# Turning the softmax blocks inside SBUF instead of through DRAM, in a fused attention and gMLP kernel

## The chip, the cores and the metric

The kernel runs on one core of a Trainium2 chip. The time is device microseconds of one execution; three executions of the kernel before gave 1901.39, 1904.52 and 1908.22 us, so the median is 1904.52 us. The engines are TensorE (PE, with its weight loads as PEld), VectorE (DVE), ScalarE (ACT), GpSimd (POOL) and SyncE (SP), which here only issues DMAs. Each engine runs its own instructions in order and waits on semaphores for the others.

## The reference

The input x (2048 x 512) is normalised by rows. Two branches read it: attention with 32 heads over the last 512 keys of a cache, and a gMLP block. The output is x plus the attention times silu of the gMLP.

```python
def _A_ref(x, k_cache, v_cache, wq, wo):
    W = min(4096, max(256, Sk // 4))                     # 512
    q = (x @ wq).reshape(B, Sq, Hq, Dh).transpose(0, 2, 1, 3)
    scores = einsum("bhqd,bhkd->bhqk", q, k_last_W) * Dh ** -0.5
    p = softmax(scores)
    o = einsum("bhqk,bhkd->bhqd", p, v_last_W)
    return o.transpose(0, 2, 1, 3).reshape(B, Sq, Hq * Dh) @ wo

def _B_ref(x, w_in, w_sp, b_sp, w_out):
    z = gelu(x @ w_in); z1 = z[..., :Fh]; z2 = layernorm(z[..., Fh:])
    g = einsum("ts,bsf->btf", w_sp, z2) + b_sp[None, :, None]
    return (z1 * g) @ w_out

xn = layernorm(x)
return x + _A_ref(xn, ...) * silu(_B_ref(xn, ...))
```

## The kernel before, in words

Everything is fp32. A product of two fp32 matrices is made of three matmuls in a fast fp32 format: each operand is split into a high part (a cast on ACT, tile names ending in `_h`) and the rest (a subtraction on DVE or POOL, names ending in `_l`), and `mm3` (lines 64 to 67) issues high x high, high x low and low x high.

**The main loop.** The attention works in 128 blocks: one head by 512 queries. A block has four steps of 128 queries, so there are 512 steps, and the program is written out by hand step by step: every engine's order is the order in which the loop at the end of the printed code calls the functions. For a block b the work is spread over many steps, each part a fixed number of steps behind the scores:

- `score(t)`: PE makes the scores of step t in a PSUM tile `ps` (pool of four), DVE finds the negated maximum `nm`, ACT makes `prob` = exp(scores + nm) with its row sums.
- `turn(t-1)`, one step later: p must have keys on partitions to be multiplied with v. DVE's transpose turns 32 x 32 pieces within a partition group only, so the groups of 32 partitions must still be exchanged. Before, the transposed pieces of two steps stand in a tile `pB`, which SP writes to DRAM (`p_dram`, 512 KB, two writes per block), and `turned(b)`, called in step 4b+7, reads it back with its groups exchanged in four transfers of 256 KB into `pL`.
- `shares(b, c)`, in step 4b+11+c (`ML` = 11): ACT casts a quarter of `pL` into `pT_h`, POOL makes `pT_l`.
- `pv(b, c)`, in step 4b+13+c (`PL` = 13): three matmuls add p times v into a PSUM bank `ps_a`; after the fourth, `pv_out` splits the sum into `oT_h` and `oT_l`.
- `outp(b, j)`, in step 4b+18+j (`OL` = 18): three matmuls with wo, and DVE adds the result, divided by the row sums, into `sacc`.

**The queries** for four blocks together, a group, are made by 42 matmuls spread over 16 steps (`q_products`, line 448), which begin `LEAD` = 13 steps ahead of the group's first score. They use three banks, a, b and c: bank b holds one product in the third to the fifth of the 16 steps, bank c two from the eighth step on, and bank a is kept for all 16 steps and let go by `qT_l` (line 728, the deferred list `late` at the end of a step) one step after the next group's products have begun. The group's banks and the banks of `pv` come from one pool of four PSUM banks, named `ps_a`; a tile of that name gets the bank that is free or the first to become free.

**SP** issues the loads of weights (`raw`, `wq`, 256 KB each, two per block on average), stores and loads of the normalised x (`x_dram`), the writes of p and the reads of p, in the order of the program. A DMA that has to wait for DVE or POOL holds up all DMAs behind it. The DMAs take eight completion semaphores in turn, and each one waits, before it is issued, until the one that had its semaphore before it, eight DMAs earlier, has landed (the waits named DMAHW in the rows further down).

Between steps 30 and 215 the second half of x is normalised, transposed and split (`later_x`), in stages that go through a ring of four tiles `rawx`; ACT writes a tile of the ring again when its store to `x_dram` has landed.

After the loop come the second half of the gMLP's first product and its spatial product (from about 1560 us on), which this change does not touch.

Of the kernel before, what the change touches and what calls it, by code (L numbers as in the profile page):

```python
# [8 lines left out]
F32 = mybir.dt.float32  # L9
F32R = mybir.dt.float32r  # L10
# [7 lines left out]
P = 128  # L18
# [10 lines left out]
NBLK = H * NQ  # L29
# [1 line left out]
SCALE = DH ** -0.5  # L31


XL, QL, ML, PL, OL = 11, 7, 11, 13, 18
T8 = NT // 2
LEAD = 13
Q = 32


# [1 line left out]
def mixer_kernel(ctx: ExitStack, tc: tile.TileContext, x, wh, w_in, w_sp, b_sp, w_out, out):  # L41
# [8 lines left out]
    nc = tc.nc  # L50
# [3 lines left out]
    dram = ctx.enter_context(tc.tile_pool(name="dram", bufs=1, space=DRAM))  # L54
# [3 lines left out]
    def rest(engine, lo, whole, hi):  # L58
        engine.tensor_tensor(lo, whole, hi.bitcast(F32), op=OP.subtract)  # L59

    late = []
# [25 lines left out]
    ap = att.enter_context(tc.tile_pool(name="ap", bufs=2))  # L87
# [6 lines left out]
    def x8(shape, dtype=F32R):  # L94
        return xp.tile(shape, dtype, name="x8")
# [18 lines left out]
    def place(key, k, early):  # L114

        if early:
            if key == ("w", 0) or k == 3:
                name = "pT" if key == ("w", 0) else "oT"
                return [ap.tile([P, 512], F32R, name=f"{name}_{a}", bufs=4 if name == "pT" else 2) for a in "hl"]
            f = (1, 2, 2)[k]  # L120
        elif key[0] == "h":
            f = k
        elif key[0] == "q":
            f = 3
        elif key[1] < 2:
# [234 lines left out]
    def z1_piece(i, n, between=lambda: None):  # L360
        z1_out(i, n, z1_product(i, n, between))


    pB = [None]
    qps, qT, pps, pD, pL, pT, oT, prob, sums = {}, {}, {}, {}, {}, {}, {}, {}, {}

    def where(b):

# [36 lines left out]
    def load_q(g):  # L405
        r = wraw[g] = wq.tile([P, 2, 512], F32, name="wq", bufs=2)
        h = 2 * g % H
        for k in range(2):
            nc.sync.dma_start(r[:, k], wh[h + k, :, 0])
# [69 lines left out]
    def turn(t):  # L479

        b, j = divmod(t, 4)
        if j % 2 == 0:
            pB[0] = ap.tile([P, 4, 2, P], F32, name="pB", bufs=3)
        nc.vector.transpose(pB[0][:, :, j % 2, :].rearrange("p a (c q) -> p a c q", q=Q),  # L486
                            prob.pop(t).rearrange("p (a c q) -> p a c q", a=4, q=Q))
        if j == 0:
            pD[b] = dram.tile([2, P, 1024], F32, name="p_dram", bufs=3)
        if j % 2:  # L490
            nc.sync.dma_start(pD[b][j // 2], pB[0].rearrange("p a j f -> p (a j f)"))
        if j == 3:
            nc.vector.reciprocal(sums[b], sums[b])

    def turned(b):
        pL[b] = ap.tile([P, 8, 256], F32, name="pL")
        of = pD.pop(b).rearrange("s (i r) (a f) -> a r (s i) f", i=4, a=4)
        for a in range(4):
            nc.sync.dma_start(pL[b][Q * a:Q * a + Q], of[a])

    def shares(b, c):
        hi = ap.tile([P, 512], F32R, name="pT_h", bufs=4)
        lo = ap.tile([P, 512], F32R, name="pT_l", bufs=4)
        p = pL[b].rearrange("p i (j f) -> p (i j) f", j=2)[:, :, Q * c:Q * c + Q]
        h, l = (t.rearrange("p (i q) -> p i q", q=Q) for t in (hi, lo))
        nc.scalar.copy(h, p)  # L506
        rest(nc.vector if 4 * b + c >= NSTEP - 10 and c % 2 else nc.gpsimd, l, p, h)
        pT[b, c] = (hi, lo)
# [6 lines left out]
    def pv_out(b, c):  # L515
        if c == 3:
            hi = ap.tile([P, 512], F32R, name="oT_h")
            lo = ap.tile([P, 512], F32R, name="oT_l")
            ps = pps.pop(b).rearrange("p (s i j q) -> p s i j q", s=2, i=4, j=2)
            h, l = (t.rearrange("p (s j i q) -> p s i j q", s=2, i=4, j=2) for t in (hi, lo))  # L520
            nc.scalar.copy(h, ps)
            for k in range(2):
                late.append((rest, nc.vector, l[:, k], ps[:, k], h[:, k]))
            oT[b] = (hi, lo)

    def outp(b, j):
# [44 lines left out]
    for g in range(1, NG):  # L571
        t0 = 16 * g - LEAD
        loads.setdefault(max(T0, t0 - 12), []).append(g)
# [72 lines left out]
    ps = ps_step.tile([P, 512], F32, name="ps_3")  # L646
# [9 lines left out]
    ps = ps_step.tile([P, 512], F32, name="ps_3")  # L656
# [4 lines left out]
    ps = ps_acc.tile([P, 512], F32, name="ps_a")  # L661
# [18 lines left out]
    for t in range(T0, T1):  # L680
        for key in loads.get(t, ()):
            if isinstance(key, int):
                load_q(key)
            else:
                load_piece(*key)
        bq, cq = divmod(t + QL, 4)
        bm, cm = divmod(t - ML, 4)
        bp, cp = divmod(t - PL, 4)
        bo, jo = divmod(t - OL, 4)
        i = t + XL  # L690
        if i < T8:
            ln_flip(i)
        if 0 <= bm < NBLK:
            shares(bm, cm)
        for f, args in todo.get(t, ()):
            f(*args)
        if 0 <= t < NSTEP:
            score(t)
        if i + 2 < T8:
            ln_apply(rows[i + 2], i + 2)  # L700
        if t in FILL:
            z1_piece(*FILL[t])
        if 0 <= bq < 4:
# [12 lines left out]
        for f, *args in q_events.get(t, ()):  # L716
            f(*args)
        if 0 <= bp < NBLK:
            pv_out(bp, cp)
        if t in DRAIN:  # L720
            z1_out(*DRAIN[t], ps)
        if 0 <= t - 1 < NSTEP:
            turn(t - 1)
        if t % 4 == 3 and 0 <= t // 4 - 1 < NBLK:
            turned(t // 4 - 1)
        while late:
            f, *args = late.pop(0)
            f(*args)  # L728
        for f, *args in ends.get(t, ()):
            f(*args)  # L730

    split_piece(("w", 2), 3, nc.vector)
    ps = z1_product(*LAST[-1])
# [276 lines left out]
```

## Time and profile before

| | |
|---|---|
| median of 3 runs | 1904.52 us (1901.39 to 1908.22) |
| profiled execution | 1907.01 us, its span 1905.1 us |
| mean granted TensorE clock of that execution | 0.991 |
| PE busy | 1820.5 us (96%) |
| DVE, POOL, ACT busy | 1403.3, 1244.3, 1179.1 us |
| DMA | 429.16 MB, mean 225 GB/s; queue of SP 79.4% of 16 engines |
| first and last maximum of scores (DVE, line 475) | 47.9 us, 1497.2 us |

The page gives shares of the whole span; the stages differ. The main loop is the stretch from about 60 to 1500 us, and in it a group of 16 steps takes 43.4 us where nothing disturbs it. In the rows of waits, "PE ps_a L65 <- DVE qT_l L728" means that PE stood idle before a matmul of line 65 that writes `ps_a`, until DVE's instruction of line 728 that writes `qT_l` had ended. PEld, the weight load, shows the same waits once more. A wait of an engine other than PE matters only where PE ends up waiting for it.

### The profile page before, as it was taken

Reading aid. Unit: us, or ns where it says so; the run is one execution under the profiler, and the core shown is the slowest. Engines: PE = TensorE matmul, PEld = TensorE weight load, DVE = VectorE, ACT = ScalarE, POOL = GpSimd, SP = SyncE. Lnnn points to the kernel's source line nnn. Section 1 sums busy time; section 2 is a strip of 40 time slices with the busy share of each in tenths; the row PEclk is TensorE's granted clock in tenths of the full one; section 3 lists DMA queues with packets and bytes.
Section 4 is the critical chain, followed back from the end, with each engine's and each line's share of the span. In section 5 each row is a group of like instructions: output and inputs, shape, how many; then the busy total and the mean of one; then the engine's idle time right before and its main releaser. Section 6 shows DMA issues by size and latency. Waiting matters only on the chain.

```text
span 1905.1 us, 28198 instructions
## 1 busy us (share of the span) xinstructions
PE 1820.5 (96%) x8658; PEld 1540.4 (81%) x8658; DVE 1403.3 (74%) x2497; ACT 1179.1 (62%) x2631; POOL 1244.3 (65%) x1185
## 2 busy tenths in 40 slices
PE   8898999999999898999999999999999999999999
PEld 7776777777787686778887877878777899999998
DVE  5687888888888787788888888888888556333433
ACT  4666677777677575667677777777677545333422
POOL 3686798798798786788878888888888435000000
PEclk9998999999999999999999999999999999999999
DMA  5798999999999889999889899988999833545543
GB/s 180 198 282 228 237 264 242 251 265 239 252 264 244 216 248 296 267 270 247 236 239 241 241 241 245 245 237 245 236 246 260 257 134 119 194 146 168 158 134 96
DMA packets 277624, 429.16 MB, mean 225 GB/s; under 512 B 22272, under 2 KB 183808, under 8 KB 276320
## 3 DMA queue, kind: packets, MB, share of 16 engines
q1 hardware_dynamic: 272864, 421.72, 79.4%
q10 hardware_dynamic: 4608, 5.64, 0.8%
q8 instruction: 68, 1.11, 0.3%
q14 instruction: 84, 0.69, 0.1%
HBM read 260.55 MB, written 166.72 MB: 224 GB/s over the span
## 4 chain that ended last, share of the span: by engine, by line
PE 73%; DMA 11%; DVE 7%; ACT 3%; POOL 3%; issue 2%; SPq 1%; ACTq 0%; POOLq 0%; DVEq 0%
PE ps_a L448 11%; PE ps L65 9%; PE ps L67 9%; PE ps L66 9%; PE ps_a L65 7%; PE ps_a L66 6%; PE ps_a L67 6%; DMA pL<-p_dram 4%; PE ps_g L66 4%; PE ps_g L67 4%; PE ps_g L65 4%; DMA p_dram<-pB 2%; DVE sacc L536 2%; DVE pB L486 1%; ACT prob L477 1%
## 5 line engine op out<-in xcount | busy, mean ns | idle before, releaser
L59 POOL TENSOR_TENSOR pT_l<-pL,pT_h 128x512 fp32r<-128x512 f32 x507 | 657.9, 1298 | 265.5 <-ACT pT_h L506 250.7
L477 ACT ACTIVATE prob<-ps,nm 128x512 f32<-128x512 f32 x512 | 352.8, 689 | 290.9 <-DVE nm L475 285.1
L536 DVE SCALAR_TENSOR_TENSOR sacc<-ps,sums,sacc 128x512 f32<-128x512 f32 x496 | 369.6, 746 | 149.2 <-PE ps L67 144.2
L506 ACT CAST pT_h<-pL 128x512 fp32r<-128x512 f32 x512 | 318.1, 621 | 130.8 <-DMA pL<-p_dram 68.3
L448 PE MATMUL ps_a<-x,x 128*128 128x512 f32 x1302 | 378.6, 391 | 7.9 <-ACT qs L455 6.9
L486 DVE STREAM_TRANSPOSE pB<-prob 128x512 f32<-128x512 f32 x512 | 359.0, 701 | 23.2 <-ACT prob L477 22.4
L475 DVE TENSOR_REDUCE nm<-ps 128x1 f32<-128x512 f32 x512 | 338.8, 662 | 8.6 <-PE ps L67 8.5
L448 PEld LDWEIGHTS ps_a<-x,x 128*128 128x128 f32 x1302 | 245.9, 189 | 61.9 <-ACT qs L455 8.3
L59 POOL TENSOR_TENSOR wl<-raw,wh 128x512 fp32r<-128x512 f32 x192 | 249.2, 1298 | 9.0 <-ACT wh L141 9.0
L65 PE MATMUL ps_a<-pT_h,wh 128*128 128x512 f32 x512 | 204.2, 399 | 46.7 <-DVE qT_l L728 42.3
L65 PE MATMUL ps<-wh,qT_h 128*128 128x512 f32 x512 | 204.0, 399 | 8.6 <-DVE sacc L536 5.1
L66 PE MATMUL ps_a<-pT_l,wh 128*128 128x512 f32 x512 | 203.0, 396 | 7.3 <-POOL pT_l L59 7.1
L67 PE MATMUL ps_a<-pT_h,wl 128*128 128x512 f32 x512 | 200.9, 392 | 0.0
L66 PE MATMUL ps<-wl,qT_h 128*128 128x512 f32 x512 | 200.9, 392 | 0.0
L65 PE MATMUL ps<-wh,oT_h 128*128 128x512 f32 x512 | 200.7, 392 | 0.0
L66 PE MATMUL ps<-wl,oT_h 128*128 128x512 f32 x512 | 200.6, 392 | 0.0
L67 PE MATMUL ps<-wh,oT_l 128*128 128x512 f32 x512 | 200.6, 392 | 0.0
L67 PE MATMUL ps<-wh,qT_l 128*128 128x512 f32 x512 | 200.6, 392 | 0.0
L66 PE MATMUL ps_g<-z_l,x 128*128 128x344 f32 x512 | 162.1, 317 | 1.3 <-POOL z_l L59 1.3
L65 PE MATMUL ps_g<-z_h,x 128*128 128x344 f32 x512 | 162.1, 317 | 0.0
L67 PE MATMUL ps_g<-z_h,x 128*128 128x344 f32 x512 | 161.9, 316 | 0.0
L65 PEld LDWEIGHTS ps_a<-pT_h,wh 128*128 128x128 f32 x512 | 96.7, 189 | 79.2 <-DVE qT_l L728 55.0
(203 smaller groups left out, 3235.3 us busy)
## 6 DMA issues: line engine op xcount, KB each, us to landing
p_dram<-pB SPq DMA_DIRECT2D x256, 512.0 KB, 5.2
pL<-p_dram SPq DMA_DIRECT2D x512, 256.0 KB, 5.8
raw<-wh SPq DMA_DIRECT2D x194, 256.0 KB, 6.7
wq<-wh SPq DMA_DIRECT2D x62, 256.0 KB, 6.1
x<-w_sp SPq DMA_DIRECT2D x60, 256.0 KB, 6.0
x_dram<-rawx SPq DMA_DIRECT2D x32, 256.0 KB, 5.6
x<-x_dram SPq DMA_DIRECT2D x28, 256.0 KB, 7.6
u_dram<-uB SPq DMA_DIRECT2D x15, 384.0 KB, 2.3
```

What stands on the lines that cost most here:

```text
L59: engine.tensor_tensor(lo, whole, hi.bitcast(F32), op=OP.subtract)
L65: nc.tensor.matmul(ps, lh, rh, start=first, stop=False)
L66: nc.tensor.matmul(ps, lh, rl, start=False, stop=False)
L67: nc.tensor.matmul(ps, ll, rh, start=False, stop=last)
L448: nc.tensor.matmul(qps[g, bank], wt["q", g, k][a][:, c * P:(c + 1) * P], X[g * 2 // H][ORDER[k]][:, b, c], start=first, stop=r == 5, skip_ ...
L475: nc.vector.tensor_reduce(nm, ps, axis=AX.X, op=OP.max, negate=True)
L477: nc.scalar.activation(prob[t], ps, AF.Exp, bias=nm, accum_out=sums[b][:, j:j + 1])
L486: nc.vector.transpose(pB[0][:, :, j % 2, :].rearrange("p a (c q) -> p a c q", q=Q), prob.pop(t).rearrange("p (a c q) -> p a c q", a=4, q=Q))
L506: nc.scalar.copy(h, p)
L536: nc.vector.scalar_tensor_tensor(at, ps, rs, at, op0=OP.mult, op1=OP.add)
```

## The change

p is turned without DRAM. The transposed pieces of all four steps of a block now stand in one `pB` (two buffers of 8 KB per partition, where there were three of 4 KB), and when the fourth is there, in step 4b+4, SP issues 16 transfers of 64 KB (32 partitions by 2 KB) from `pB` straight into `pL`, one for each pair of a source group and a target group. `turned` is gone. The casts come 9 steps behind the scores and no longer 11, `pv` 11 and no longer 13, `outp` 16 and no longer 18. `pT_h` and `pT_l` have three buffers each and no longer four. The queries of a group are begun 14 steps ahead, not 13. The layout of `pL` makes the eviction of `pv` simpler: one subtraction of 128 x 512 in place of two of 128 x 256.

```diff
-XL, QL, ML, PL, OL = 11, 7, 11, 13, 18
+XL, QL, ML, PL, OL = 11, 7, 9, 11, 16
 T8 = NT // 2
-LEAD = 13
+LEAD = 14
...
-                name = "pT" if key == ("w", 0) else "oT"
-                return [ap.tile([P, 512], F32R, name=f"{name}_{a}", bufs=4 if name == "pT" else 2) for a in "hl"]
+                name = "oT" if k == 3 else "pT"
+                return [ap.tile([P, 512], F32R, name=f"{name}_{a}", bufs=3 if name == "pT" else 2) for a in "hl"]
...
+    SWAPS = [(0, 0), (2, 2), (1, 1), (3, 3), (0, 1), (2, 3), (1, 0), (3, 2),
+             (0, 2), (2, 0), (1, 3), (3, 1), (0, 3), (2, 1), (1, 2), (3, 0)]
...
-        if j % 2 == 0:
-            pB[0] = ap.tile([P, 4, 2, P], F32, name="pB", bufs=3)
-        nc.vector.transpose(pB[0][:, :, j % 2, :].rearrange("p a (c q) -> p a c q", q=Q),
+        if j == 0:
+            pB[0] = ap.tile([P, 4, 4, P], F32, name="pB")
+        nc.vector.transpose(pB[0][:, :, j, :].rearrange("p a (c q) -> p a c q", q=Q),
                             prob.pop(t).rearrange("p (a c q) -> p a c q", a=4, q=Q))
-        if j == 0:
-            pD[b] = dram.tile([2, P, 1024], F32, name="p_dram", bufs=3)
-        if j % 2:
-            nc.sync.dma_start(pD[b][j // 2], pB[0].rearrange("p a j f -> p (a j f)"))
         if j == 3:
+            pL[b] = ap.tile([P, 4, 512], F32, name="pL")
+            for a, i in SWAPS:
+                nc.sync.dma_start(pL[b][Q * a:Q * a + Q, i], pB[0][Q * i:Q * i + Q, a].rearrange("r j f -> r (j f)"))
             nc.vector.reciprocal(sums[b], sums[b])

-    def turned(b):
-        pL[b] = ap.tile([P, 8, 256], F32, name="pL")
-        of = pD.pop(b).rearrange("s (i r) (a f) -> a r (s i) f", i=4, a=4)
-        for a in range(4):
-            nc.sync.dma_start(pL[b][Q * a:Q * a + Q], of[a])
...
-        hi = ap.tile([P, 512], F32R, name="pT_h", bufs=4)
-        lo = ap.tile([P, 512], F32R, name="pT_l", bufs=4)
-        p = pL[b].rearrange("p i (j f) -> p (i j) f", j=2)[:, :, Q * c:Q * c + Q]
+        hi = ap.tile([P, 512], F32R, name="pT_h", bufs=3)
+        lo = ap.tile([P, 512], F32R, name="pT_l", bufs=3)
+        p = pL[b].rearrange("p i (j f) -> p (i j) f", j=4)[:, :, Q * c:Q * c + Q]
...
-            for k in range(2):
-                late.append((rest, nc.vector, l[:, k], ps[:, k], h[:, k]))
+            late.append((rest, nc.vector, l, ps, h))
...
-        if t % 4 == 3 and 0 <= t // 4 - 1 < NBLK:
-            turned(t // 4 - 1)
```

How this moves instructions is seen at two places. The first is SP's order in the main loop. Before, this stood there for a little over one block (a name ahead of "<-" is what a DMA writes, the brackets say which semaphores it waits for: DVE's, POOL's, or one of the eight of the DMAs):

```order
L491 DMA p_dram<-pB 128x1024 [waits DMAHW6_49,DVE_49]
L499 DMA pL<-p_dram 32x8x256 [waits DMAHW7_49,DMAHW3_49,Pool_49]
L499 DMA pL<-p_dram 32x8x256 [waits DMAHW0_49]
L499 DMA pL<-p_dram 32x8x256 [waits DMAHW1_49]
L499 DMA pL<-p_dram 32x8x256 [waits DMAHW2_49]
L102 DMA raw<-wh 128x512
L491 DMA p_dram<-pB 128x1024 [waits DMAHW4_49,DVE_49]
L491 DMA p_dram<-pB 128x1024 [waits DMAHW5_49,DVE_49]
```

After the change the loads of two blocks stand together between two rows of 16 transfers each, of which the first waits for DVE's transpose and for POOL's last reading of the `pL` that it overwrites:

```order
L102 DMA raw<-wh 128x512 [waits DMAHW5_49]
L102 DMA raw<-wh 128x512 [waits DMAHW6_49]
L411 DMA wq<-wh 128x512 [waits DMAHW7_49]
L411 DMA wq<-wh 128x512 [waits DMAHW0_49]
L102 DMA raw<-wh 128x512 [waits DMAHW1_49,Pool_49]
L493 DMA pL<-pB 32x512 [waits DMAHW2_49,DVE_49,Pool_49]
L493 DMA pL<-pB 32x512 [waits DMAHW3_49]
L493 DMA pL<-pB 32x512 [waits DMAHW4_49]
```

So per block SP issues 16 transfers of p and no longer 6, and the loads that came between them now stand before or behind whole rows of 16.

The second place is PE's order in the third of a group's 16 steps of query products, in the middle of the run. Before, scores, then the last matmul on bank a and the first on bank b, then the first matmul of a block's `pv`, which waits for DVE:

```order
L65 MATMUL ps_3_14948<-wh1_14637,qT_h_14831 128x512 [waits DVE_49]
L66 MATMUL ps_3_14948<-wl1_14638,qT_h_14831 128x512
L67 MATMUL ps_3_14948<-wh1_14637,qT_l_14832 128x512
L448 MATMUL ps_a_14881<-x8_8565,x8_737 128x512
L448 MATMUL ps_a_14957<-x8_8638,x8_737 128x512
L65 MATMUL ps_a_14959<-pT_h_14865,wh2_14707 128x512 [waits DVE_49]
L66 MATMUL ps_a_14959<-pT_l_14866,wh2_14707 128x512 [waits Pool_49]
L67 MATMUL ps_a_14959<-pT_h_14865,wl2_14708 128x512
```

After the change, the corresponding `pv` (`ps_a_15650`) begins one step earlier than bank b, and waits for ACT's cast of its own operand; the DVE wait stands at the first matmul on bank b (`ps_a_15684`):

```order
L450 MATMUL ps_a_15614<-x8_8971,x8_707 128x512 x3
L65 MATMUL ps_a_15650<-pT_h_15575,wh2_15465 128x512 [waits Activation_49]
L66 MATMUL ps_a_15650<-pT_l_15576,wh2_15465 128x512 [waits Pool_49]
L67 MATMUL ps_a_15650<-pT_h_15575,wl2_15466 128x512
L65 MATMUL ps_3_15654<-wh3_15354,oT_h_15493 128x512 [waits Activation_49]
L66 MATMUL ps_3_15654<-wl3_15355,oT_h_15493 128x512
L67 MATMUL ps_3_15654<-wh3_15354,oT_l_15494 128x512
L65 MATMUL ps_3_15674<-wh1_15385,qT_h_15552 128x512 [waits DVE_49]
L66 MATMUL ps_3_15674<-wl1_15386,qT_h_15552 128x512
L67 MATMUL ps_3_15674<-wh1_15385,qT_l_15553 128x512
L450 MATMUL ps_a_15614<-x8_8971,x8_707 128x512
L450 MATMUL ps_a_15684<-x8_9053,x8_707 128x512 [waits DVE_49,PE_49]
```

Before, the DVE instruction waited for is `qT_l` of line 728, at the end of the step just before. Now it is `oT_l` of a block whose `pv` ended two steps before, at the end of that step, so a whole step of PE's work lies between.

More of the change, by code (lines that the diff above doesn't have):

```diff
@@ L364, in mixer_kernel @@
     pB = [None]
-    qps, qT, pps, pD, pL, pT, oT, prob, sums = {}, {}, {}, {}, {}, {}, {}, {}, {}
+    SWAPS = [(0, 0), (2, 2), (1, 1), (3, 3), (0, 1), (2, 3), (1, 0), (3, 2),
+             (0, 2), (2, 0), (1, 3), (3, 1), (0, 3), (2, 1), (1, 2), (3, 0)]
+    qps, qT, pps, pL, pT, oT, prob, sums = {}, {}, {}, {}, {}, {}, {}, {}
     def where(b):
@@ L518, in pv_out @@
             lo = ap.tile([P, 512], F32R, name="oT_l")
-            ps = pps.pop(b).rearrange("p (s i j q) -> p s i j q", s=2, i=4, j=2)
-            h, l = (t.rearrange("p (s j i q) -> p s i j q", s=2, i=4, j=2) for t in (hi, lo))
+            ps = pps.pop(b).rearrange("p (i j q) -> p i j q", i=4, j=4)
+            h, l = (t.rearrange("p (j i q) -> p i j q", i=4, j=4) for t in (hi, lo))
             nc.scalar.copy(h, ps)
-            for k in range(2):
-                late.append((rest, nc.vector, l[:, k], ps[:, k], h[:, k]))
+            late.append((rest, nc.vector, l, ps, h))
             oT[b] = (hi, lo)
```

## The prediction

> **What bounds the kernel now.** I read the page first, then PE's waits, then the timeline around the longest of them, then stretches of the main loop, and last the DMAs. The page says that PE is the engine to look at: in the second row each digit is the busy share of a fortieth of the span in tenths.
>
> ```profile
> PE 1820.5 (96%) x8658; PEld 1540.4 (81%) x8658; DVE 1403.3 (74%) x2497; ACT 1179.1 (62%) x2631; POOL 1244.3 (65%) x1185
> PE   8898999999999898999999999999999999999999
> DMA  5798999999999889999889899988999833545543
> ```
>
> So all that can be won is PE's idle time, 1905.1 - 1820.5 = 85 us, and what the clock loses. The view of PE's waits (us in total, times, longest) says where the idle time is:
>
> ```profile
> PE ps_a L65 <- DVE qT_l L728: 42.3, 30, 7.8
> PE ps_a L66 <- POOL pT_l L59: 7.1, 13, 1.1
> PE ps_a L448 <- ACT qs L455: 6.9, 2, 6.3
> PE ps L65 <- DVE sacc L536: 6.4, 10, 1.3
> PE ps_a L65 <- ACT pT_h L506: 4.4, 3, 1.8
> PE ps L65 <- ACT prob L477: 3.1, 2, 2.5
> ```
>
> Half of it is one wait, 30 times, once in nearly every group of 16 steps: the first matmul of a block's `pv` waits for the bank that `qT_l` lets go. The timeline at such a place, undisturbed:
>
> ```profile
> 1116.62 0.70 DVE L486 STREAM_TRANSPOSE pB<-prob 128x512 f32<-128x512 f32 x1
> 1117.30 0.66 DVE L728 SCALAR_TENSOR_TENSOR qT_l<-ps_a,qT_h 128x512 fp32r<-128x512 f32 x1
> 1116.43 0.61 PE L448 MATMUL ps_a<-x,x 128*128 128x512 f32 x2
> 1118.02 0.50 PE L65 MATMUL ps_a<-pT_h,wh 128*128 128x512 f32 x1 [0.97 <-DVE qT_l L728]
> ```
>
> DVE is not late here; the bank is asked for too early, so PE loses 0.97 us in every group. The rest of the 42.3 us, 42.3 - 30 x 0.97 = 13 us, and much of the other rows come from a few long stalls:
>
> ```profile
> 149.61 0.62 ACT L506 CAST pT_h<-pL 128x512 fp32r<-128x512 f32 x1 [7.99 <-DMA pL<-p_dram]
> 154.40 0.80 PE L65 MATMUL ps_a<-pT_h,wh 128*128 128x512 f32 x1 [7.84 <-DVE qT_l L728]
> 640.58 0.41 ACT L309 CAST rawx<-rawx 128x256 fp32r<-128x256 f32 x1 [8.09 <-DMA x_dram<-rawx]
> 642.20 0.80 PE L448 MATMUL ps_a<-x,x 128*128 128x512 f32 x1 [6.29 <-ACT qs L455]
> ```
>
> Each begins with ACT waiting for a DMA that landed late, p coming back from DRAM or a store of x; the exponentials queue behind on ACT, DVE starves, and PE stops. They cost a second time. In the stretches (the figure after POOL's is the granted clock, then the DMAs' busy share, then GB/s) the clock drops where they are:
>
> ```profile
> 60.00:200.00 140.00, 125.28 (x531) 100.34 (x529) 104.95 (x188) 91.34 (x216) 103.98 (x102) 0.95 0.91 249
> 600.00:800.00 200.00, 179.71 (x751) 144.16 (x750) 152.22 (x273) 126.97 (x296) 149.28 (x141) 0.96 0.95 258
> 800.00:1000.00 200.00, 194.23 (x843) 158.55 (x843) 169.69 (x301) 140.14 (x326) 166.63 (x155) 0.99 0.91 248
> 1000.00:1400.00 400.00, 390.68 (x1706) 318.73 (x1705) 342.03 (x603) 283.85 (x658) 333.97 (x311) 1.00 0.91 242
> ```
>
> Lost clock: 0.05 x 140 + 0.04 x 200 + 0.01 x 200 = 17 us. DVE (342 of 400), POOL (334) and the DMAs (0.91) are close behind PE; the DMAs are the ones that come late.
>
> **The change, part by part.** *The bank wait.* With LEAD 14 and PL 11, `pv` begins one step sooner against the query products, takes a bank that has been free for long, and the bank after it is let go a whole step before it is asked for; a step is 43.4 / 16 = 2.7 us, more than the 0.97 us missing. Bounds: 0 (the wait comes back elsewhere in the group) and -42.3 us. I take -42.3, the row itself, if p is there in time.
>
> *Is p there in time?* Between the moment when `pB` is complete and `pL` free, and the first cast, there were 7 steps with a write and a read in them; now there are 5 with 16 transfers. The time at hand, from the rows of the undisturbed group at 1017 us: the tightest place is from the end of POOL's `pT_l` in step 336 (1021.24; the same step's `pT_l` will free the older `pL`) to ACT's cast of step 341, 8.4 us; the widest is from the end of DVE's transpose in step 340 (1030.02) to the cast of step 345, 12.1 us.
>
> ```profile
> 1019.94 1.30 POOL L59 TENSOR_TENSOR pT_l<-pL,pT_h 128x512 fp32r<-128x512 f32 x1
> 1029.67 0.64 ACT L506 CAST pT_h<-pL 128x512 fp32r<-128x512 f32 x1
> 1029.32 0.70 DVE L486 STREAM_TRANSPOSE pB<-prob 128x512 f32<-128x512 f32 x1
> 1042.11 0.64 ACT L506 CAST pT_h<-pL 128x512 fp32r<-128x512 f32 x1
> ```
>
> ACT may be later than that at no cost: here it waited 2.60 us for the first cast of a block (the row names PE, which had long been done; the block's `pL` is what came last), and PE has no wait between 945 and 985 us.
>
> ```profile
> 961.93 0.62 ACT L506 CAST pT_h<-pL 128x512 fp32r<-128x512 f32 x1 [2.60 <-PE ps_a L448]
> ```
>
> What the 16 transfers need, no row shows: no transfer in this trace goes from SBUF to SBUF. The nearest rows (median us from issue to landing, KB each; then the time in SP's queue of one issue, min/median/max ns):
>
> ```profile
> p_dram<-pB SPq DMA_DIRECT2D x256, 512.0 KB, 5.2
> pL<-p_dram SPq DMA_DIRECT2D x512, 256.0 KB, 5.8
> uL<-u_dram SPq DMA_DIRECT2D x60, 96.0 KB, 2.1
> L499 SPq DMA_DIRECT2D pL<-p_dram x512: 302/448/1700, 67.8 to 1514.8; - x171
> L903 SPq DMA_DIRECT2D uL<-u_dram x60: 308/424/1437, 1621.5 to 1879.6; - x60
> ```
>
> `uL` is nearest: also 32 partitions wide, 96 KB, four in a row. It lands in 2.1 us where the DMAs are half idle; 5.8 us is the far end, four times the bytes with the DMAs at 0.91. The new state lies near the first: per block 2 MB of p are moved now (2 x 512 + 4 x 256 KB), then 1 MB, and two loads of 256 KB stay, so 2.5 MB become 1.5 MB and the share falls from 0.91 to about 0.55. I take 2.1 to land and 0.37 per issue (between 0.30 and 0.45): 16 x 0.37 + 2.1 = 8.0 us, ends 6.9 and 9.3 with the same landing. Against 8.4 to 12.1 us that is in time, and the slow end is 0.9 us late where 2.6 us cost nothing. So late p, hence `pT_h` 4.4 and `pT_l` 7.1 us, is half gone: -6 (0 to -11.5). Of the clock's 17 us I take back half: -9 (0 to -17).
>
> The Trainium skill speaks against this part: its page "DMA: Bandwidth & Descriptors", section "Rules for kernel authors", says that small transfers should be joined into large ones and that two transfers to different halves of the partitions just run one behind the other; its table of loads in the section "Bandwidth" has 138 GB/s for 64 KB. By that, as an estimate, the 1 MB of a block would take 7.6 us and 2.1 to land, 9.7 us, 1.3 us late at the tightest place, with the same sum. No run here shows such transfers.
>
> *SP.* Per block 18 issues by 0.37 = 6.7 us of 10.9 (43.4 / 4): not the bound. But its order is one queue. A store of `rawx` written in the step after a row of 16 is issued some 6 us later than now, and ACT waits for its tile. Today these waits are:
>
> ```profile
> ACT rawx L309 <- DMA x_dram<-rawx: 22.5, 4, 8.1
> ```
>
> Of the four stages of `later_x`, two now have their store one or two steps behind the start of a row of 16 (in steps 157 and 110), two do not. One of today's four cost PE 6.3 us; I take one more: +6 (ends 0 and 2 x 6.3 = +12.6). The weight loads wait behind a row too, but are issued 6 steps, 16 us, ahead, and get over 6 us of delay.
>
> *Three buffers of `pT`.* A cast now needs the `pv` of the step before to be done, no longer of the step before that. PE does `outp` and the next scores after it, six matmuls; the 1000 to 1400 row gives 390.68 / 1706 = 0.23 us each, so the buffer is free 1.4 us before the step's scores end, and ACT rarely casts sooner. Bounds 0 and 0.5 us in two steps of 16, on ACT, which is idle there: 0. *One subtraction for two* (`oT_l`): DVE, not the bound, 0. *Two steps less at the end:* PE has no gap there, 0:
>
> ```profile
> 1500.00:1560.00 60.00, 60.00 (x348) 56.02 (x346) 29.94 (x54) 24.80 (x49) 15.97 (x16) 1.00 0.60 207
> ```
>
> **The sum,** against the profiled execution's own 1907.0 us (span 1905.1 and 1.9 around it): -42.3 - 6 - 9 + 6 = -51, that is 1856 us. The median of the runs shown is 2.5 us lower, so I forecast 1853 us. Ends of this case: all of it and also the rows of `sacc`, `qs` and `prob`, -42.3 - 11.5 - 17 - 6.9 - 6.4 - 3.1 = -87, 1818 us; only the regular waits, 30 x 0.97 = -29, 1876 us.
>
> **The rivals.** *The transfers land late* (slower). Each of SP's DMAs waits for the landing of the one eight before. If one takes L to land, the ninth of a row goes out at L, the 16th lands at 2L + 7 x 0.37. ACT can stand 8.4 + 2.6 = 11 us, so the point that decides is L = 4.2 us. At 4.8 us 18 issues, L/8 apart, fill the 10.9 us of a block, and beyond it SP is the bound: at 5.2 us (`p_dram`'s row) 11.7 us per block, 0.8 x 128 = +105, 2010 us; at 5.8 us (`pL`'s) 13.1, 2.2 x 128 = +275, 2180 us. For it speak those two rows; against it the `uL` row and the lower DMA load. The rule of the Trainium skill quoted above, if it held in full, would push this way.
>
> *The wait only moves* (no change to speak of). The bank's wait is gone, but the stores and the x loads around step 230 stall ACT behind the rows of 16 as p does now: -29 regular, +12.6 stores, +10 for two stalls more with their clock: 1898 us. For it: the 640 us row. Against it: less DMA traffic. Here 1885 to 1912 us.
>
> *DVE or POOL becomes the bound:* with the loop 3% shorter DVE has 342 us of work in 388: still idle time; a chance is not given.
>
> **How the numbers follow.** Forecast 0.62, transfers late 0.22, the wait moves 0.16. A measurement of this kernel tells about 0.3%, 6 us, from no change. The moved wait splits into 0.07 faster, 0.05 same, 0.04 slower; so faster 0.69, same 0.05, slower 0.26. The range starts at 1818 and goes up to 1940, past the moved wait and into the late transfers, of which the larger part, 0.16, is left out; the likeliest case alone has 1818 to 1880.
>
> **What the profile will show.** Right: no row of PE waiting for `qT_l`; groups of about 42.5 us; DMA share 0.5 to 0.6; `pL<-pB` landing in 2 to 3 us; 0.3 to 0.45 us per issue; clock 0.995. Wrong: `pL<-pB` landing over 4 us, ACT waiting for it in every block, and SP's issues back to back.

## The result: 9% slower, with SP's queue as the new bound

The kernel after takes 2081.19 us (median of 4 runs, 2080.31 to 2090.43), the kernel before, measured beside it, 1903.47 us: a ratio of 1.094 (95% interval 1.090 to 1.098). The forecast was 1853 us. The profiled execution has a span of 2088.6 us against 1905.1 before, 183.5 us more.

Its page, with the rows that answer to those of before (engines; PE's and the DMAs' share by fortieths of the span; SP's DMA queue; the chain that ended last, by engine and by line):

```profile
PE 1895.7 (91%) x8658; PEld 1583.1 (76%) x8658; DVE 1400.0 (67%) x2369; ACT 1174.6 (56%) x2631; POOL 1242.7 (59%) x1185
PE   8888889789888898899998999999999899999999
DMA  4455555545555555655545555555455562544442
q1 hardware_dynamic: 195040, 287.58, 50.1%
SPq 38%; PE 28%; DMA 19%; POOL 8%; issue 5%; ACT 1%; DVE 1%; ACTq 0%; POOLq 0%
pL<-pB SPq DMA_DIRECT2D x2048, 64.0 KB, 2.0
```

The 183.5 us split in two. PE's idle time went from 84.6 to 2088.6 - 1895.7 = 192.9 us (+108.3). PE's busy time went from 1820.5 to 1895.7 us (+75.2) for the same 8658 matmuls. DVE, ACT and POOL do no more work than before, and the DMAs are half idle: their queue fell from 79.4% to 50.1%. The chain names SPq, the queue in which SP issues DMAs, with 38%. A transfer lands 2.0 us after its issue in the median, as forecast.

The clock is where the busy time went: the mean granted clock fell from 0.991 to 0.951, and 1820.5 x 0.991 / 0.951 = 1897 us, against 1895.7 measured. By stretches (the granted clock stands behind POOL's figure, then DMA share and GB/s):

```profile
200.00:400.00 200.00, 172.78 (x707) 136.43 (x706) 147.50 (x255) 122.59 (x289) 141.47 (x137) 0.93 0.53 139
600.00:800.00 200.00, 178.15 (x746) 141.18 (x745) 150.87 (x257) 124.94 (x295) 149.71 (x144) 0.97 0.55 142
1000.00:1400.00 400.00, 369.05 (x1527) 296.21 (x1528) 308.75 (x514) 256.48 (x598) 305.50 (x284) 0.95 0.52 131
```

Between 1000 and 1400 us, where only the loop's own work is left, PE did 1706 matmuls at a clock of 1.00 before and does 1527 at 0.95 now.

The waits of after (us in total, times, longest) show the old wait gone and another in its place:

```profile
ACT pT_h L501 <- DMA pL<-pB: 298.2, 66, 9.4
POOL pT_l L59 <- ACT pT_h L501: 257.4, 142, 7.6
DVE pB L488 <- DMA pL<-pB: 177.7, 67, 7.6
...
PE ps_a L65 <- ACT pT_h L501: 88.2, 36, 5.2
...
ACT rawx L309 <- DMA x_dram<-rawx: 47.4, 4, 14.6
...
PE ps L65 <- ACT prob L479: 40.1, 10, 9.1
PE ps_a L66 <- POOL pT_l L59: 35.4, 53, 0.9
```

Before, ACT's row of waiting for p was this:

```profile
ACT pT_h L506 <- DMA pL<-p_dram: 68.3, 26, 8.0
```

PE has no row with `qT_l` left. Now PE waits for `pT_h` (ACT's cast of p), ACT for the transfers, and DVE for `pB` to be read out. The timeline at one place shows the three in a row; the brackets give the idle time before, and what ended it:

```profile
1001.54 0.71 DVE L488 STREAM_TRANSPOSE pB<-prob 128x512 f32<-128x512 f32 x1 [4.87 <-DMA pL<-pB]
1001.55 0.62 ACT L501 CAST pT_h<-pL 128x512 fp32r<-128x512 f32 x1 [7.03 <-DMA pL<-pB]
...
1002.23 0.79 PE L65 MATMUL ps_a<-pT_h,wh 128*128 128x512 f32 x1 [3.08 <-ACT pT_h L501]
```

Why are transfers late that land in 2.0 us? SP's own rows say it (start, length, line, how many in a run without a gap):

```profile
999.71 10.00 SPq L493 DMA_DIRECT2D pL<-pB  x16
1009.75 1.55 SPq L102 DMA_DIRECT2D raw<-wh  x3
1011.86 20.94 SPq L493 DMA_DIRECT2D pL<-pB  x32
1032.85 1.08 SPq L102 DMA_DIRECT2D raw<-wh  x2
1033.97 0.90 SPq L411 DMA_DIRECT2D wq<-wh  x2
1034.98 0.38 SPq L102 DMA_DIRECT2D raw<-wh  x1
1035.46 22.45 SPq L493 DMA_DIRECT2D pL<-pB  x32
1057.96 1.55 SPq L102 DMA_DIRECT2D raw<-wh  x3
1059.89 0.51 SPq L493 DMA_DIRECT2D pL<-pB  x1
```

(The last line is the start of the next 32; the view ends there.) SP issues almost without a pause. Sixteen issues take 10.0 us and 32 take 20.94 or 22.45, which is 0.63 to 0.70 us each. Four blocks with their eight loads of weights take 1059.89 - 1011.86 = 48.0 us, 12.0 for one block, and the groups of four blocks from about 1000 us on take 46 to 49. Taken one by one, an issue has these times in the queue (min/median/max ns):

```profile
L493 SPq DMA_DIRECT2D pL<-pB x2048: 507/588/1871, 62.5 to 1700.8; - x187
```

SP's waits in the stretch from 1000 to 1400 us, before and then after, say the same from the other side. Before, SP stood still for DVE's `pB` in 167.9 of 400 us; now in 0.2, so the data are there before SP has time for them:

```profile
SPq L491 <- DVE pB L486: 167.9, 37, 5.0
SPq L499 <- DMA p_dram<-pB: 38.9, 17, 4.1
```

```profile
SPq L493 <- DMA raw<-wh: 15.8, 27, 1.6
...
SPq L493 <- DVE pB L488: 0.2, 1, 0.2
```

### The profile page after: what moved, and what is told of

It is laid out like the page before. It is cut to its first block, busy times and chain, and to the rows that moved or that the text cites. A ratio compares the mean times of both kernels' runs of the same rounds, so it can differ in the third digit from the quotient of the medians.

```text
span 2088.6 us, 29901 instructions
## 1 busy us (share of the span) xinstructions
PE 1895.7 (91%) x8658; PEld 1583.1 (76%) x8658; DVE 1400.0 (67%) x2369; ACT 1174.6 (56%) x2631; POOL 1242.7 (59%) x1185
## 3 DMA queue, kind: packets, MB, share of 16 engines
q1 hardware_dynamic: 195040, 287.58, 50.1%
## 4 chain that ended last, share of the span: by engine, by line
SPq 38%; PE 28%; DMA 19%; POOL 8%; issue 5%; ACT 1%; DVE 1%; ACTq 0%; POOLq 0%
SPq L493 34%; DMA raw<-wh 13%; PE ps_g L66 4%; PE ps_g L67 4%; PE ps_g L65 4%; POOL pT_l L59 4%; DMA pL<-pB 3%; PE ps_a L66 2%; PE ps_a L67 2%; PE ps_a L65 2%; SPq L102 2%; PE ps L65 2%; PE ps L66 2%; PE ps L67 2%; POOL wl L59 2%
## 5 line engine op out<-in xcount | busy, mean ns | idle before, releaser
L501 ACT CAST pT_h<-pL 128x512 fp32r<-128x512 f32 x512 | 317.2, 620 | 401.4 <-DMA pL<-pB 298.2
L450 PE MATMUL ps_a<-x,x 128*128 128x512 f32 x1302 | 389.4, 401 | 0.3 <-DVE oT_l L59 0.3
L450 PEld LDWEIGHTS ps_a<-x,x 128*128 128x128 f32 x1302 | 253.8, 195 | 56.6 <-PE ps_a L450 0.7
L65 PE MATMUL ps_a<-pT_h,wh 128*128 128x512 f32 x512 | 211.8, 414 | 88.4 <-ACT pT_h L501 88.2
L65 PE MATMUL ps<-wh,qT_h 128*128 128x512 f32 x512 | 211.5, 413 | 45.0 <-ACT prob L479 39.9
L66 PE MATMUL ps_a<-pT_l,wh 128*128 128x512 f32 x512 | 215.6, 421 | 35.6 <-POOL pT_l L59 35.4
L65 PE MATMUL ps<-wh,oT_h 128*128 128x512 f32 x512 | 207.3, 405 | 10.5 <-ACT oT_h L516 9.6
L67 PE MATMUL ps_a<-pT_h,wl 128*128 128x512 f32 x512 | 207.0, 404 | 0.0
L66 PE MATMUL ps<-wl,qT_h 128*128 128x512 f32 x512 | 206.9, 404 | 0.0
L66 PE MATMUL ps<-wl,oT_h 128*128 128x512 f32 x512 | 206.4, 403 | 0.0
L67 PE MATMUL ps<-wh,oT_l 128*128 128x512 f32 x512 | 206.3, 403 | 0.0
```

The costliest lines, as they stand in the source:

```text
L65: nc.tensor.matmul(ps, lh, rh, start=first, stop=False)
L66: nc.tensor.matmul(ps, lh, rl, start=False, stop=False)
L67: nc.tensor.matmul(ps, ll, rh, start=False, stop=last)
L450: nc.tensor.matmul(qps[g, bank], wt["q", g, k][a][:, c * P:(c + 1) * P], X[g * 2 // H][ORDER[k]][:, b, c], start=first, stop=r == 5, skip_ ...
```

## The experiments

The theory after the result: the bank wait went as forecast, but SP can't issue 16 transfers and its loads in the time in which PE does a block. Rivals: the exchange between partition groups is slow by its bytes; the shorter distance of 9 steps is too short whatever SP does; the first half of the loop is slow by its own work. "Quiet half" below means the groups behind the last loads and stores of x, in the kernel after those from about 1000 us on, and a group's time goes from its first maximum of scores on DVE to the next group's. The kernel before took 1906.79 us beside the first four kernels, 1908.14 beside the next four, and 1906.96 beside the last three.

### The bank wait alone

```diff
-LEAD = 13
+LEAD = 12
```

This is the kernel before, p through DRAM, with only the start of the queries moved a step later. `pv` then stands to the query products as it does in the change: `LEAD` + `PL` is 25 in both, and 26 before.

> The kernel before with LEAD 12 in place of 13 and nothing else; p still goes through DRAM. Theory: the regular 0.97 us of PE per group is the bank asked for a step too early, whatever p does; then that row of PE's waits is gone and the time falls by 29 to 42 us, to 1861 to 1875 us. Rival: the wait only moves to another bank or another engine; then 1897 to 1909 us, with a row of 25 to 40 us elsewhere among PE's waits.

Measured: 1853.13 us (1851.81 to 1857.26), a ratio of 0.972 (0.969 to 0.975). PE's longest waits, and the stretch of the quiet half:

```profile
PE ps_a L65 <- ACT pT_h L506: 8.9, 4, 4.0
```

```profile
1000.00:1400.00 400.00, 400.00 (x1766) 331.24 (x1765) 354.77 (x626) 294.25 (x684) 347.53 (x321) 1.00 0.93 251
```

PE has no row with `qT_l` left and no gap at all in this stretch, and a group takes 42.2 us where it took 43.0 to 44.7. The step is worth 1906.79 - 1853.13 = 54 us, and the transfers weren't needed to get it. In the profiled executions PE's idle time falls by 84.6 - (1850.0 - 1807.6) = 42.2 us, as much as the row of 42.3 had, and its busy time by another 12.9. The expectation had counted the first only, so the time lies below its 1861 to 1875 us. What shortened the busy time isn't shown: the mean clock is 0.991 in both.

### Four transfers of 128 partitions in place of 16

```diff
-            for a, i in SWAPS:
-                nc.sync.dma_start(pL[b][Q * a:Q * a + Q, i], pB[0][Q * i:Q * i + Q, a]...)
+            for i in range(4):
+                nc.sync.dma_start(pL[b][:, i], pB[0][:, i]...)
```

> The changed kernel with 4 transfers of 128 x 512 per block, SBUF to SBUF as before and the same bytes, in place of 16 of 32 x 512; the exchange between partition groups is left out, so p stays in its groups. Theory (number of issues on SP): SP needs under 4 us per block and the time is 1820 to 1865 us. Rival (the bytes going SBUF to SBUF, or the time left for them, are the matter): above 1950 us. The median issue tells whether the 0.59 us belong to SBUF on both sides (again 0.5 to 0.6) or to the 32 partitions (0.33, as the write of 128 partitions to DRAM had).

Measured: 1818.69 us (1817.57 to 1820.56), 0.954 (0.951 to 0.957). The issues one by one, and a block of them in SP's rows:

```profile
L493 SPq DMA_DIRECT2D pL<-pB x512: 464/600/2136, 61.2 to 1419.4; - x171
```

```profile
1003.90 2.40 SPq L493 DMA_DIRECT2D pL<-pB  x4
```

The time is at the edge of the 1820 to 1865 us expected. An issue of four times the bytes costs the same 0.6 us. The same bytes go from SBUF to SBUF at the same distance of 9 steps, with the same buffers of `pT` and the same `LEAD`, and ACT has no row of waiting for p left: those parts of the change do no harm, and 1818.7 us is about what the change would bring if SP were free. What differs is the number of issues, and that nothing crosses a partition group; the next runs separate these.

### Sixteen issues with half the bytes each

```diff
-                nc.sync.dma_start(pL[b][Q * a:Q * a + Q, i], pB[0][Q * i:Q * i + Q, a]...)
+                nc.sync.dma_start(pL[b][Q * a:Q * a + Q, i, :256], pB[0][Q * i:Q * i + Q, a, :2]...)
+            nc.sync.dma_start(pL[b][:, :, 256:], pB[0][:, :, 2:]...)
```

> The kernel after, where each of the 16 transfers carries half its bytes (32 partitions by 1 KB) and the other half goes in one transfer of 128 partitions straight across, so that half of the exchange between groups is left out and the output is not the reference's. Bytes are the same, issues are 17 and not 16. Theory 'the number of issues sets it': an issue costs 0.5 us and more whatever it carries, SP stays back to back, and one issue more per block is 0.6 x 128 = 80 us: 2080 to 2200 us, with 0.5 to 0.6 us in the row of the issues. Theory 'the bytes between partition groups set it' (an issue is long because it waits for the engines to take its bytes): an issue of half the bytes costs about half, 0.3 us, a row takes some 6 us, and the time is like that of 10 transfers: 1830 to 1900 us.

Measured: 2208.62 us (2206.59 to 2217.1), 1.158 (1.155 to 1.161). The issues of 32 KB, and SP's rows:

```profile
L493 SPq DMA_DIRECT2D pL<-pB x2048: 507/588/1640, 58.1 to 1816.2; - x187
```

```profile
1019.80 10.32 SPq L493 DMA_DIRECT2D pL<-pB  x16
1030.21 0.66 SPq L494 DMA_DIRECT2D pL<-pB  x1
1030.98 11.49 SPq L493 DMA_DIRECT2D pL<-pB  x16
```

With half the bytes crossing between groups an issue costs the same 507 and 588 ns to the nanosecond, and the time rises by 127 us for the one issue more per block (1.0 us for each of 128, more than the 0.66 of the issue itself, and 9 us above the range expected). So the bytes of a transfer don't set its price, and leaving out half of the exchange doesn't help either; what is left is the count.

### Ten and thirteen issues

Two, or one, of the four source groups go in one transfer of 128 partitions; the others still go in fours. With two:

```diff
+            for i in range(2):
+                nc.sync.dma_start(pL[b][:, i], pB[0][:, i]...)
             for a, i in SWAPS:
-                nc.sync.dma_start(...)
+                if i >= 2:
+                    nc.sync.dma_start(...)
```

> The same with 10 transfers per block, two of them of 128 x 512; half of the exchange is left out. Theory of the threshold: SP needs 7.8 us of 10.55, the row lands 10 x 0.63 + 2 = 8.3 us after its start, in time everywhere, 1818 to 1835 us. Rival with the straight line: 1950 us.

> The changed kernel with 13 transfers per block in place of 16: one of 128 x 512 takes the place of four of 32 x 512, the same bytes; in that quarter the exchange between groups is left out. Theory (SP's queue is the bound above a threshold): a block takes SP 13 x 0.63 + 2.25 x 0.5 + 0.4 = 9.7 us, PE 42.2 / 4 = 10.55 us (groups of 42.2 us in the run with whole transfers), so SP is no longer the bound; most groups come down to 42.2 to 43 us and the time to 1825 to 1870 us, all but a little of the 262 us between 4 and 16 transfers. Rival (each transfer costs the same share, since each delays p): a straight line from 1819 us at 4 to 2081 us at 16 gives 2015 us.

Measured: 1845.93 us with 10 (1844.63 to 1847.62; 0.968, 0.966 to 0.970) and 1911.91 us with 13 (1908.66 to 1919.42; 1.002, 1.000 to 1.004). SP's waits between 1000 and 1400 us, with 10 and then with 13:

```profile
SPq L493 <- DVE pB L488: 110.9, 39, 4.0
```

```profile
SPq L493 <- DVE pB L488: 11.0, 18, 1.1
```

| issues of p per block | SP's wait for `pB`, us of 400 | PE's matmuls in these 400 us | time, us |
|---|---|---|---|
| 4 | 263.3 | 1769 | 1818.69 |
| 10 | 110.9 | 1766 | 1845.93 |
| 13 | 11.0 | 1749 | 1911.91 |
| 16 (after) | 0.2 | 1527 | 2081.19 |

So there is a threshold. As long as SP has slack, the quiet half runs at PE's own pace (42.2 us a group with 4 and with 10); with 13 the slack is just used up (41.8 to 44.0 us), and with 16 the loop runs at SP's pace. ACT's wait for p goes the same way: no row with 4, then 23.7, 92.9 and 298.2 us. The 6 issues from 4 to 10 cost 27 us, the 3 from 13 to 16 cost 169. Both times miss what the threshold theory gave (1818 to 1835 with 10, 1825 to 1870 with 13), and the loss is in the first half: between 200 and 800 us PE did 2604 matmuls with 4 issues, 2477 with 10, 2345 with 13, and 2128 in the kernel after. SP isn't full there even with 13; it waits for `pB` in 48.4 of these 600 us. What grows with the count there is ACT's wait for p (none with 4, 19.4 us with 10, 32.2 with 13) and its wait for the stores of x, which stand behind the rows of p: 16.8 us with 4, 29.6 with 10, 38.8 with 13, 47.4 with 16. The last experiment takes them out of that order.

### Sixteen transfers read from DRAM

```diff
+            pD = dram.tile([P, 4, 512], F32, name="p_dram", bufs=3)
+            nc.sync.dma_start(pD, pB[0].rearrange("p a j f -> p a (j f)"))
             for a, i in SWAPS:
-                nc.sync.dma_start(pL[b][Q * a:Q * a + Q, i], pB[0][Q * i:Q * i + Q, a]...)
+                nc.sync.dma_start(pL[b][Q * a:Q * a + Q, i], pD[Q * i:Q * i + Q, a])
```

> The changed kernel with p written to DRAM in one transfer of 1 MB per block and read back in 16 of 64 KB, 32 x 512, right behind it. It measures the issue of the same shape with DRAM as the source: 0.30 to 0.45 us if the 0.59 us go with SBUF on both sides, 0.5 to 0.6 us if they go with the shape. SP stands still for the write's landing in each block, so the time itself is above 2081 us by any theory.

Measured: 2411.88 us, one run. The issues, a row of 16, and SP's longest wait between 1000 and 1400 us:

```profile
L495 SPq DMA_DIRECT2D pL<-p_dram x2048: 302/419/1803, 66.1 to 2021.5; - x187
```

```profile
1001.59 7.29 SPq L495 DMA_DIRECT2D pL<-p_dram  x16
```

```profile
SPq L495 <- DMA p_dram<-pB: 158.2, 27, 8.9
```

A transfer of the same shape costs 0.419 us to issue when it comes from DRAM, 0.588 when it comes from SBUF; a row of 16 takes 7.29 us and not 10. The kernel is slower for another reason: SP stands before the reads until the write of 1 MB has landed (6.0 us after its issue). From `pB` to the last landing that makes 6.0 + 7.3 + 2.0 = 15.3 us, where five steps of PE's pace are 5 x 42.2 / 16 = 13.2 us. So there are two ways to be late, and they read differently: here SP waits, in the kernel after SP works.

### A quarter of the issues by ACT

```diff
+                if n < 12:
+                    nc.sync.dma_start(*args)
+                else:
+                    by_act.append((t + 2 + (n - 12) // 2, args))
...
+        while by_act and by_act[0][0] <= t:
+            nc.scalar.dma_start(*by_act.pop(0)[1])
```

> The changed kernel, with 4 of the 16 transfers of a block issued by ACT one and two steps later, 12 by SP. Theory: SP's time per issue (0.59 us median, 0.63 with the gap, 64 of them and 9 loads per group, 46 us where PE needs 42.5) is the bound; with 12 SP needs 12 x 0.63 + 2.25 x 0.47 = 8.6 us of 10.7 per block, and the time falls below the kernel before, to 1840 to 1900 us, unless ACT, which gets 4 x 0.6 = 2.4 us more per block, becomes the bound itself. Rival: the transfers land too late whoever issues them, since 5 steps are too few; then it stays above 2000 us.

Measured: 1993.12 us (1991.85 to 1997.28), 1.045 (1.042 to 1.048), in between what the two theories gave. ACT's issues, and what ACT waits for then:

```profile
L696 ACTq DMA_DIRECT2D pL<-pB x512: 513/517/1449, 61.5 to 1593.5; - x171
```

```profile
ACT prob L479 <- DMA pL<-pB: 112.5, 35, 5.3
```

SP's wait for `pB` between 1000 and 1400 us:

```profile
SPq L495 <- DVE pB L488: 50.0, 27, 3.1
```

Taking four issues from SP gives back 88 us, which speaks for the theory, and SP has slack again. But the groups of the quiet half still take 44 to 47 us, so SP is no longer what holds them: an issue costs ACT 0.517 us too, and ACT stands still in front of its DMAs, with the exponentials behind them. The Trainium skill, page "DMA: Bandwidth & Descriptors", section "Issuing engines are not separate DMA queues", says that issuing from several engines saves only the time of issuing, "which is usually small relative to the DMA itself". The first part agrees with this run, where the time falls by 88 us; the second doesn't fit this kernel, where a row of 16 is 10.0 us of issuing and 2.0 us to the landing of the last.

### Part of p inside SBUF, part through DRAM

```diff
+            pD = dram.tile([P, 2, 512], F32, name="p_dram", bufs=3)
+            nc.sync.dma_start(pD, pB[0][:, 2:].rearrange("p a j f -> p a (j f)"))
...
+                if a < 2:
+                    nc.sync.dma_start(pL[b][Q * a:Q * a + Q, i], pB[0][Q * i:Q * i + Q, a]...)
+            of = pD.rearrange("(i r) a f -> a r i f", i=4)
+            for a in range(2, 4):
+                nc.sync.dma_start(pL[b][Q * a:Q * a + Q], of[a - 2])
```

This is the half; the quarter has `a < 1` and three reads.

> The changed kernel with half of each block's p (target groups 0 and 1) going inside SBUF in 8 transfers and half through DRAM, one write of 512 KB and two reads of 256 KB; everything is computed. SP per block: 8 x 0.63 + 0.35 + 2 x 0.45 + 1.1 = 7.4 us of 10.55, no bound; the reads go out behind the 8 transfers, some 5.5 us after the row's start, and land 4 to 5.6 us later, 9.5 to 11 us against 8.4 to 12.1 at hand and 2.6 more at no cost. Theory: 1825 to 1865 us. Rival (DRAM's way in 5 steps is late): 1880 to 1960 us with waits of ACT for pL in most blocks.

> The same with a quarter inside SBUF (4 transfers) and three quarters through DRAM (a write of 768 KB, three reads of 256 KB); everything is computed. SP 5.3 us per block. Less work for SP than with 8, more on the DMAs: the reads wait for the write's landing, some 5 us, and land 4 to 5.6 us later, 10.5 to 12 us. If SP's time alone counts: 1820 to 1850 us, at or below the half and half. If the way through DRAM is what comes late: above it, 1860 to 1950 us.

Measured: 1881.26 us with the half (1879.19 to 1885.07; 0.987, 0.985 to 0.989) and 1867.39 us with the quarter (1863.81 to 1871.01; 0.979, 0.977 to 0.982). Both compute all of p, with 11 and 8 issues per block, and are faster than the kernel before by 1 and 2%. The half lies at the lower end of its rival's range, though ACT waits for p from DRAM in 12 places only and not in most blocks, and the quarter fits neither of its two: it is below the half, but above 1860 us. In the quiet half both run at nearly PE's pace, with 1756 and 1762 matmuls between 1000 and 1400 us, so SP has slack again; the loss is in the first half. The count isn't all there: the run with 10 issues and no way through DRAM has 1845.93 us. Neither beats the 1853 us of the first experiment, either. In the quarter the longest wait of ACT for p is one for DRAM, `pL<-p_dram` with 54.1 us in 19 times, where the first experiment has 29.6. That 9 steps leave less time for a write and a read than 11 did would explain it, and isn't shown.

### The stores of x issued by ACT

```diff
         def store(*ks):
             for k in ks:
-                nc.sync.dma_start(xd[1, k]...
+                nc.scalar.dma_start(xd[1, k]...
```

Once in the kernel after, and once in the kernel of the first experiment (`LEAD` 12, p through DRAM).

> The kernel after, with the stores of x to x_dram in the first half of the main loop (line 314) issued by ACT and no longer by SP; the same work otherwise. Theory 'SP is the bound, and what stands behind its rows comes late': in the quiet second half nothing changes (groups of 47 to 50 us), in the first half the wait of ACT for x_dram (47.4 us in 4) falls below 20 us and the groups come down from 51 to 58 us towards 48 to 52: 2020 to 2060 us. Theory 'the first half is slow because of its own work on POOL and ACT': the groups stay above 51 us, 2070 to 2100 us.

> The kernel before with queries begun 12 steps ahead (1853 us), and the stores of x to x_dram (line 314) issued by ACT. Theory 'in the first half ACT waits for stores that stand in SP's queue' (21.2 us in 4 waits there): the waits fall below 8 us and the time comes down to 1830 to 1848 us. Theory 'the store is late because its data or the DMAs are late, not the queue': the waits stay, and ACT now also stands still before a store that waits for POOL: 1850 to 1870 us.

Measured: 2039.21 us (2036.82 to 2041.44; 1.069, 1.066 to 1.071) and 1850.91 us (1843.26 to 1853.0; 0.969, 0.966 to 0.971). The wait for the stores in the first of them, and its stretches:

```profile
ACT rawx L309 <- DMA x_dram<-rawx: 6.8, 4, 2.4
```

```profile
200.00:800.00 600.00, 549.85 (x2277) 432.21 (x2276) 465.72 (x797) 388.97 (x914) 460.93 (x442) 0.97 0.57 148
1000.00:1400.00 400.00, 371.03 (x1545) 298.63 (x1544) 310.77 (x518) 258.49 (x603) 307.52 (x286) 0.96 0.53 133
```

Taking 32 issues from SP in the first half removes 42 us, nearly all of it there (2277 matmuls and not 2128 between 200 and 800 us; the wait 47.4 is now 6.8), and next to nothing in the quiet half (1545 and not 1527). So in the first half, too, SP's queue made a good part of the loss: the stores stood behind the rows of p. In the kernel through DRAM, where SP has slack, the same edit moves the wait from 21.2 to 16.1 us only, and the time by 2 us, less than the runs scatter: there the expectation of 1830 to 1848 us is missed, and SP's order is at most a small part of what holds the stores up. They land 5.9 us after their issue from SP and 6.0 from ACT.

What no run has: the transfers inside SBUF with the old distance of 11 steps. By the SP rows it wouldn't help, as more distance gives SP no time; that is argued, not shown.

## Why the prediction was wrong, point by point

- **The bank wait, -42.3 us: right.** The row is gone in the kernel after. Alone, the step takes 42.2 us from PE's idle time, and 54 us in all.
- **Landing, 2.1 us: right** (2.0).
- **The issue, 0.37 us, 16 in 8.0 us with the landing: wrong, and this is the step that failed.** An issue of this kind takes 0.588 us (least 0.507) and comes every 0.63 to 0.70, so the row takes 10.0 us or more and is complete after 12.0, at the wide end of the time at hand (12.1) and far beyond the tight one (8.4, or 11.0 with the 2.6 us that cost nothing). The range of 0.30 to 0.45 was taken from loads out of DRAM. It stood even below the medians of the rows quoted (0.424 and 0.448), and left out that the source is another memory, though the same text said that no row shows such a transfer. The trace of before had a dearer issue on the same queue, the stores of x, in a row that the prediction didn't use:

```profile
L314 SPq DMA_DIRECT2D x_dram<-rawx x32: 524/526/1762, 211.7 to 665.6; - x32
```

  Had 0.526 been the far end, the row would have been 16 x 0.526 + 2.1 = 10.5 us: 2.1 late at the tight place, and only 0.5 left of the 2.6 us counted as free. SP's sum would have been 16 x 0.526 + 2 x 0.45 = 9.3 us of 10.9. That is close, but it still isn't the bound; the dearest kind of issue in that trace is, by the median, still below the 0.588 measured.
- **"SP: 18 issues by 0.37 = 6.7 us of 10.9: not the bound": wrong by the same term.** Measured are 48.0 us for four blocks, 12.0 for one, where PE needs 42.2 / 4 = 10.55 once the bank wait is gone. The error of 0.26 us per issue, and more where they come slower, is multiplied by 16 and turns a queue that was thought to have over a third of its time free into the bound. The gain on PE made it worse: the time that a block leaves to SP falls from 10.9 to 10.55 us.
- **Stores of x, +6 us: right in kind, wrong in size.** ACT's wait for them rose from 22.5 to 47.4 us, and the experiment that takes them off SP gives 42 us.
- **Late p -6 and the clock -9: wrong in sign.** Both rest on p being in time. ACT's wait for p rose from 68.3 to 298.2 us, and the lower clock took 75.2 us more of PE's time. The clock's loss goes with the stalls: in the runs with four and with ten transfers the clock of the quiet half is 1.00.
- **Three buffers of `pT`, one subtraction, two steps less at the end, 0 us: right.** The run with four transfers has them all and takes 1818.7 us.
- **The rival "the transfers land late": right in its effect, wrong in its cause.** It named SP as the bound, ACT waiting in every block and SP back to back, but made all of it hang on the landing (over 4.2 us, through the eight completion semaphores), which is 2.0. Its price of 2010 us stood at 11.7 us per block, close to the 12.0 measured, but that is luck, as it was made of a landing of 5.2 us. Of the rest, up to 2081, the stores of x make 42 us; what makes the other 29 isn't split by a run. It let the landing vary and left the price of an issue at 0.37.
- **The rule quoted there,** from the Trainium skill, page "DMA: Bandwidth & Descriptors", section "Rules for kernel authors", to join small transfers, pointed the right way. By the bytes, with the table of its section "Bandwidth", the estimate came to 9.7 us per row, against 12.0 measured; but half the bytes in as many transfers aren't faster, so the cost here is the count, not the bandwidth. The Trainium skill, page "Perfetto Trace Analysis", section "What "DMA-bound" means", has the case as it turned out: one of its kinds is the sequencer that issues, whose track is then solid with DMA slices that are descriptor generation and not data movement. The rows of SP agree (32 issues in 20.94 us, the DMAs at 0.52).

## What to carry to other kernels

A DMA has two prices, the time that the issuing queue needs for it and the time to its landing, and half the bytes left the first as it was here: count the issues per unit of the loop, multiply by the dearest issue that the queue shows, and set it against the pace that the loop will have after the gain. Here that gives 9.3 us of 10.55, not over, but so near that the price of the new issue wanted measuring first. If what is issued now differs in kind from every row (other memory, other pattern), the range of its price is at least that of all rows of the queue, not of the one that looks alike; here the measured one lay above them all. And when a change has a part that removes a wait and a part that moves work, see first whether the first can be had alone: one constant (`LEAD` 12) gives 1853 us here, better than both kernels, and the stores on ACT add nothing clear to it (1851).

## What the runs showed of the hardware that was not expected

- The price of an issue on SP goes with the kind of DMA; where only the size differs, 32 or 64 KB inside SBUF, it is the same (min/median ns):

| DMA | KB | ns |
|---|---|---|
| SBUF to DRAM, 128 partitions, whole rows (`p_dram`, before) | 512 | 319/327 |
| DRAM to SBUF, 32 partitions by 2 KB (16 reads) | 64 | 302/419 |
| SBUF to DRAM, rows cut into pieces (`x_dram<-rawx`, before) | 256 | 524/526 |
| SBUF to SBUF, 32 partitions by 2 KB (after) | 64 | 507/588 |
| SBUF to SBUF, 32 partitions by 1 KB | 32 | 507/588 |
| SBUF to SBUF, 128 partitions by 2 KB | 256 | 464/600 |
| SBUF to SBUF, 128 partitions by four pieces of 1 KB | 512 | 663/664 |

  The same shape is 0.17 us dearer out of SBUF than out of DRAM. But a store to DRAM in pieces is nearly as dear, so "SBUF on both sides" isn't the whole of it; which property of the instruction sets the price isn't settled. The median also depends on what stands before it in the queue: the transfer of 128 partitions by 2 KB that heads each row in the run with 13 has 507/517, and the reads of 256 KB from DRAM, 302/448 before, have 311/576 behind eight transfers inside SBUF in the run with the half.
- In a full queue the issues follow each other in 0.63 to 0.70 us, more than their own median of 0.588.
- A transfer from SBUF to SBUF lands in 2.0 us, and 32 KB (1.9) hardly sooner than 64 KB; 128 partitions by 2 KB land in 2.5. Beside p going through DRAM the 64 KB land in 2.3 (the half) and 3.2 us (the quarter).
